# The first x tile's second slab by a DMA transpose, and W1's second block in another queue

## The chip, the cores and the metric

The kernel runs on one core of one Trainium2 chip. The core has five engines that run side by side and wait for one another through semaphores: TensorE (PE, with PEld for its weight loads), VectorE (DVE), ScalarE (ACT), GpSimd (POOL) and SyncE (SP). SP, ScalarE and POOL can issue DMAs; all DMAs of the core run on its 16 DMA engines. The metric is the time of one execution in device microseconds, lower is better. Times in this document are in microseconds unless something else is said.

## The reference

The input x has 2048 rows (tokens) of 640 features. Two branches are computed from it and mixed by a gate for each token:

```python
g = _sigmoid((x * gate_w).sum(-1, keepdims=True))
# branch A: a diagonal state-space layer with complex states
Bu = jnp.einsum("bld,pd->blp", x + 0j, B_bar)
for t in range(L):
    h = Lam_bar[None, :] * h + Bu[:, t, :]
y = 2.0 * jnp.einsum("blp,dp->bld", hseq, Cmat).real + x * Dskip[None, None, :]
# branch B: a dense layer with gelu, 640 -> 1728 -> 640
h = _gelu(jnp.einsum("bsd,df->bsf", x, w1) + b1)
b = jnp.einsum("bsf,fd->bsd", h, w2) + b2
out = g * a + (1 - g) * b
```

All inputs and the output are bfloat16.

## The kernel before, in words

The tokens are cut into four tiles of 512. For each tile TensorE computes the first dense layer (`m1`, L670: 13 column blocks of 128 of W1's 1728, five k steps each), the input projection of the states (`bproj`, L713), the second dense layer (L937, and L800 for the last tile) and the output projection of the states (L986, and L849 for the last tile). ScalarE evacuates the accumulators, with gelu for the dense layer. VectorE rotates and scans the states (`ssm`) and combines the branches.

TensorE contracts over partitions, so it needs x transposed, with the features on the partitions: `xT[q]` holds tile q as five slabs of 128 features by 512 tokens. Most slabs come from DRAM by a DMA transpose (`xtrans`, L340). For the first tile the slabs k < KN, here KN = 2, come in another way: the two plain loads `xna0` and `xna1` bring 256 tokens each of the first KN*128 features (L370), TensorE transposes them in blocks of 128 x 128 against an identity matrix (L426, `xt0` to `xt3`), and VectorE copies them from the accumulator bank into `xT[0]` (L432, `xc0` to `xc3`).

W1 comes in pieces. `w1load(k, queue, priority)` loads 128 rows (one k step) of the first 1024 columns, 256 KB: block 0 from ScalarE's queue (L387), blocks 1 to 4 from SP's. The remaining 704 columns follow in two loads of all rows (L378, 480 and 400 KB). After these, SP issues the transposed loads of the B weights, the next x tiles, W2 and the C weights. Each DMA has its own semaphore.

ScalarE's queue begins with W1's block 0, the single-row load `b1b` (the tail of b1, L391), and the loads of four sets of rows (Lambda's real and imaginary parts, log_dt, b1). They land in the tile `rows`, which TensorE transposes in one go (`cols`, L453). From these columns a serial chain on VectorE and ScalarE (L458, L463, L476, L483 to L497) makes the tables of the state rotation. The same columns hold b1, the bias of the gelu, so that the first gelu (L657) comes behind this chain in ScalarE's queue.

The first dense layer of the first tile has an order of its own, `m1_first` (L638 to L652). TensorE starts with six matmuls on constants (`warm`, L414), which need no data, then the transposes `xt0` and `xt1`, one more matmul on a constant (`fill`, L439), and then the first eight column blocks of W1, bank by bank, k step by k step. The k = 0 step of the first six blocks is done on token halves, first on tokens 0 to 255 and then on 256 to 511, since the halves of x arrive apart. Block 7 waits until bank 7, which the transposes use, is free.

```python
steps = [(0, jf, h) for h in range(2) for jf in range(6)] + [(k, jf, None) for k, jf in seq if k or jf > 5]
```

The order on each engine is not written out by hand. Each operation is recorded with `op(name, engine, duration, reads, writes, fn, prio)`, and a list scheduler (`Sched.order`) takes, on each engine, among the operations that are ready by its own estimated durations, the one with the lowest priority number. TensorE's main operations have running numbers from `pe_prio()`; others have fixed ones (20.5 for `cols`).

Of the kernel before, what the change touches and what calls it, by code (L numbers as in the profile page):

```python
# [184 lines left out]
def bass_gated_mix__ssm_conv_s5__dense_activation_gelu__prompt_kernel(  # L185
# [18 lines left out]
    _, S, D = A_x.shape  # L204
# [3 lines left out]
    KD = D // 128  # L208
# [17 lines left out]
    with ExitStack() as es:  # L226
# [4 lines left out]
        xT = [SB(f"xT_{i}", [128, KD, 512], BF16) for i in range(NQ)]  # L231
# [11 lines left out]
        cols = SB("cols", [128, 3 * KP + NF], FP32)  # L243
# [10 lines left out]
        ident = SB("ident", [128, 128], BF16)  # L254
# [53 lines left out]
        op = pr.op  # L308
# [17 lines left out]
        def d_mm(n):  # L326
            return n / 2400.0 + 0.004
# [31 lines left out]
        def w1load(k, eng, prio, reads=()):  # L359
            edges = [0] + ([WSPLIT[k] * 128] if k in WSPLIT else []) + [FW]  # L360
            for i, (f0, f1) in enumerate(zip(edges, edges[1:])):
                load(f"w1_{k}{i}", eng, f"l_w1{k}{i}", W1sb[:, k, f0:f1], B_w1[k * 128:(k + 1) * 128, f0:f1], [("w1", k, i)], prio=prio + 0.1 * i, lat=2.6, reads=reads)
# [1 line left out]
        def w1tok(k, jf):  # L364
            return ("w1", k, int(jf >= WSPLIT.get(k, NW)))

        KN = 2

        for h in range(2):
            load(f"xna{h}", "sp", f"l_xna{h}", xn[0][:, 2 * h:2 * h + 2, 0:KN * 128],  # L370
                 x2[h * 256:(h + 1) * 256, 0:KN * 128].rearrange("(c p) d -> p c d", p=128), [("xna", h)], 0.2 * h, dur=0.45, lat=2.0 + 0.4 * h)
        w1load(1, "sp", 1)
        for k in range(KN, KD):
            xtrans(0, range(k, k + 1), 2 * k, 1.15)
            w1load(k, "sp", 2 * k + 1)
        FM = FW + 3 * 128
        for i, (f0, f1) in enumerate(((FW, FM), (FM, F))):
            load(f"w1_r{i}", "sp", f"l_w1r{i}", W1sb[:, :, f0:f1], B_w1[:, f0:f1].rearrange("(k p) f -> p k f", p=128), [("w1", "r", i)], prio=20 + i, lat=5.0)  # L378
# [5 lines left out]
            return inc("pool", nc.gpsimd.memset(rows[:, :], 0.0))  # L384

        op("rz", "pool", 0.2, (), list(ROWS) + ["b1b", "rz"], f_rz, prio=-90)
        w1load(0, "act", -110, reads=["rz"])  # L387
        for i, (nm, (r0, src)) in enumerate(ROWS.items()):
            src = src.rearrange("(k p) -> k p", p=128)
            load(nm, "act", "l_" + nm, rows[r0:r0 + src.shape[0], :], src, [nm], prio=-100 + i, dur=0.4)  # L390
# [25 lines left out]

        op("warm", "pe", 2.7, (), [("bank", 4)], f_warm, prio=-1000)

        for i, (k, c0, c1) in enumerate(((0, 0, 2), (1, 0, 2), (0, 2, 4), (1, 2, 4))):
            bank = (7, 6, 7, 6)[i]  # L420
            pt = PS[bank][:, :].bitcast(BF16)[:, 0:(c1 - c0) * 128]

            def f_xt(k=k, pt=pt, c0=c0, c1=c1):
                t = None
                for c in range(c0, c1):
                    t = nc.tensor.transpose(pt[:, (c - c0) * 128:(c - c0 + 1) * 128], xn[0][:, c, k * 128:(k + 1) * 128], ident[:, :])  # L426
                return inc("pe", t)

            op(f"xt{i}", "pe", 0.11 * (c1 - c0), [("xna", c0 // 2), "ident"], [("bank", bank)], f_xt, prio=-990 + i if i < 2 else 3.1 + 0.1 * i)

            def f_xc(k=k, pt=pt, c0=c0, c1=c1):
                return inc("dve", nc.vector.tensor_copy(out=xT[0][:, k, c0 * 128:c1 * 128], in_=pt))  # L432

            op(f"xc{i}", "dve", 0.42, [("bank", bank)], [("xT", 0, k, c0)], f_xc, prio=-2000 + i)

        def f_fill():
            t = None
            for _ in range(1):
                t = nc.tensor.matmul(PS[3][:, 0:256], one.broadcast_to([128, 128]), one.broadcast_to([128, 256]), start=True, stop=True)  # L439
            return inc("pe", t)  # L440

        op("fill", "pe", 0.11, [("xna", 0), "ident"], [("bank", 3)], f_fill, prio=-900)

        XK0 = [[("xT", 0, k)] for k in range(KD)]
        XK0[0] = [("xT", 0, 0, 0), ("xT", 0, 0, 2)]
        XK0[1] = [("xT", 0, 1, 0), ("xT", 0, 1, 2)]
        XT = {q: [("xT", q, k) for k in range(KD)] for q in range(1, NQ)}
        XT[0] = [t for x in XK0 for t in x]

# [2 lines left out]
        def f_cols():  # L452
            return inc("pe", nc.tensor.transpose(psC, rows[:, :], ident[:, :]))  # L453

        op("cols", "pe", 0.3, list(ROWS) + ["b1b", "ident"], [("bank", 7)], f_cols, prio=20.5)

        def f_cols1():
            return inc("dve", nc.vector.tensor_copy(out=cols[:, :], in_=psC[:, 0:RT + 1]))  # L458
# [179 lines left out]
        def m1_first():  # L638
            late = [(0, NW - 1), (1, NW - 1)]
            seq = [(k, jf) for k in range(KD) for jf in range(NW) if (k, jf) not in late]  # L640
            i = seq.index((2, NW - 1))
            seq[i:i] = late
            steps = [(0, jf, h) for h in range(2) for jf in range(6)] + [(k, jf, None) for k, jf in seq if k or jf > 5]
            for k, jf, h in steps:
                t0, t1 = (0, 512) if h is None else (256 * h, 256 * h + 256)

                def f_mm(jf=jf, k=k, t0=t0, t1=t1):
                    return inc("pe", nc.tensor.matmul(PS[jf][:, t0:t1], W1sb[:, k, jf * 128:(jf + 1) * 128], xT[0][:, k, t0:t1],  # L648
                                                      start=(k == 0 and t0 == 0), stop=(k == KD - 1), skip_group_check=jf < 6))

                op(f"m1_0_{jf}_{k}_{t0}", "pe", d_mm(t1 - t0), (XK0[k] if h is None else XK0[k][h:h + 1]) + [w1tok(k, jf)], [("bank", jf)],
                   f_mm, prio=pe_prio())  # L652
            for jf in range(NW):
                ctr["bank"] += 1

                def f_ge(jf=jf):
                    return inc("act", nc.scalar.activation(Gl[0][:, jf, :], PS[jf][:, :], ACT.Gelu_apprx_tanh, bias=b1col[:, jf:jf + 1]))  # L657

                op(f"ge_0_{jf}", "act", d_act(512), [("bank", jf), "b1col"], [("gl", 0, jf)], f_ge, prio=10)
# [442 lines left out]
```

## Time and profile before

| | us |
|---|---|
| median of 3 runs | 212.86 (212.53 to 212.92) |
| the profiled execution | 212.88 |
| its span, first to last instruction | 211.6 |
| TensorE busy | 208.8 |
| VectorE busy | 190.1 |
| ScalarE busy | 103.1 |

The span is what the trace covers; the profiled execution's own time is 1.3 longer. Matmuls are pipelined, and the ends of their records are modelled, so consecutive matmuls overlap in the trace: the distance between two starts is what one costs. Operations of TensorE that the text names are found in the trace by their line: L414 the matmuls on constants, L426 the transposes of x, L439 the filler, L453 the transpose of the rows, L648 the first dense layer of the first tile for its first eight column blocks, L670 the rest of it. A DMA has two times: that of its issue on a queue, and that at which its data has landed.

### The profile page before, as it was taken

What the parts mean: (1) busy time and instruction counts of PE and PEld (TensorE: products, weight loads), DVE (VectorE), ACT (ScalarE), POOL (GpSimd) and SP (SyncE); (2) the same over time, 40 slices, a digit from 0 to 9 for tenths busy, and PEclk for the clock granted to TensorE, in tenths of its full rate; (3) what the DMA queues carried; (4) which work ended last, traced back from release to release, by engine and by line L of the source; (5) the groups of instructions that cost most, each with busy time, mean ns of one, the idle gap of its engine ahead of it and who ended that gap; (6) DMA issues with size and microseconds to landing.
All of it is one profiled execution on the core that took longest, in us unless ns stands there. A gap on an engine that the chain in (4) does not pass through costs nothing.

```text
span 211.6 us, 2759 instructions
## 1 busy us (share of the span) xinstructions
PE 208.8 (99%) x1106; PEld 105.2 (50%) x1106; DVE 190.1 (90%) x240; ACT 103.1 (49%) x177; POOL 4.2 (2%) x12
## 2 busy tenths in 40 slices
PE   8999999999999999999999999999999999999996
PEld 4544444444564444444464444444446444567775
DVE  2399999999999999999999999899999999499744
ACT  1399556678850353556680063456660027623330
POOL 1000000030000000000100000000010000000000
DMA  6999999999700020066174000007553000005251
GB/s 162 240 270 125 205 207 201 382 168 181 178 0 3 0 50 0 0 71 152 28 62 112 3 0 0 0 2 77 125 107 115 0 3 0 0 0 105 67 142 62
DMA packets 48536, 19.08 MB, mean 90 GB/s; under 512 B 41484, under 2 KB 47244, under 8 KB 48524
## 3 DMA queue, kind: packets, MB, share of 16 engines
q1 hardware_dynamic: 46720, 17.33, 39.8%
q0 software_dynamic: 1600, 1.32, 4.7%
q10 hardware_dynamic: 204, 0.27, 0.4%
q8 instruction: 8, 0.13, 0.3%
q14 instruction: 4, 0.03, 0.1%
HBM read 8.41 MB, written 2.63 MB: 52 GB/s over the span
## 4 chain that ended last, share of the span: by engine, by line
PE 99%; DVE 0%; issue 0%
PE ps L670 22%; PE ps L713 20%; PE ps L937 20%; PE ps L986 15%; PE ps L800 7%; PE ps L849 5%; PE ps L648 4%; PE ps L414 1%; PE ps L691 1%; PE ps L948 1%; PE ps L426 0%; PE ps L814 0%; DVE W1sb L883 0%; PE ps L439 0%; PE ps L453 0%
## 5 line engine op out<-in xcount | busy, mean ns | idle before, releaser
L670 PE MATMUL ps<-xT,W1sb 128*128 128x512 bf16 x220 | 48.1, 379 | 0.0
L753 DVE TENSOR_TENSOR_SCAN W<-atab,V 128x1280 bf16<-128x1280 f32 x16 | 44.3, 2811 | 0.3
L713 PE MATMUL ps<-xT,BT 128*128 128x512 bf16 x200 | 43.8, 379 | 0.0
L937 PE MATMUL ps<-Gl,W2sb 128*128 128x512 bf16 (+1 forms) x234 | 42.7, 344 | 0.0
L677 ACT ACTIVATE Gl<-ps,cols 128x512 bf16<-128x512 f32 x44 | 29.8, 695 | 15.5 <-PE ps L670 15.5
L670 PEld LDWEIGHTS ps<-xT,W1sb 128*128 128x128 bf16 x220 | 21.5, 98 | 26.0
L986 PE MATMUL ps<-Hb,CT 128*128 128x512 bf16 x150 | 32.9, 379 | 0.0
L937 PEld LDWEIGHTS ps<-Gl,W2sb 128*128 128x128 bf16 x234 | 22.9, 98 | 19.3
L713 PEld LDWEIGHTS ps<-xT,BT 128*128 128x128 bf16 x200 | 19.5, 98 | 23.7 <-ACT Gt L699 0.4
L722 ACT ACTIVATE U<-ps 128x512 bf16<-128x512 f32 x40 | 23.6, 596 | 14.8 <-PE ps L713 14.7
L955 ACT ACTIVATE E1T<-ps,cols 128x512 bf16<-128x512 f32 (+1 forms) x18 | 9.4, 624 | 36.0 <-PE ps L948 36.0
L986 PEld LDWEIGHTS ps<-Hb,CT 128*128 128x128 bf16 x150 | 14.5, 98 | 17.9 <-issue 0.6
L994 ACT ACTIVATE E2T<-ps 128x512 bf16<-128x512 f32 x15 | 9.1, 604 | 13.6 <-PE ps L986 13.6
L800 PE MATMUL ps<-W2sb,Gl 128*128 128x320 bf16 x104 | 14.8, 299 | 0.0
L622 DVE SCALAR_TENSOR_TENSOR trf<-xn,gwb 128x640 bf16<-128x640 bf16 x16 | 13.2, 823 | 0.4
L503 DVE TENSOR_TENSOR V<-V,W 128x1280 bf16<-128x1280 bf16 x16 | 12.5, 821 | 0.3
L503 DVE TENSOR_TENSOR Hb<-Hb,V 128x1280 bf16<-128x1280 bf16 x16 | 12.5, 821 | 0.3
L503 DVE TENSOR_TENSOR V<-mr,U 128x2560 bf16<-128x2560 bf16 x8 | 11.9, 1492 | 0.3
L800 PEld LDWEIGHTS ps<-W2sb,Gl 128*128 128x128 bf16 x104 | 10.1, 98 | 4.3 <-issue 0.3
L503 DVE TENSOR_TENSOR Hb<-c,W 128x2560 bf16<-128x2560 bf16 x8 | 11.9, 1490 | 0.2
L503 DVE TENSOR_TENSOR V<-s,W 128x2560 bf16<-128x2560 bf16 x8 | 11.9, 1484 | 0.0
L503 DVE TENSOR_TENSOR W<-mi,U 128x2560 bf16<-128x2560 bf16 x8 | 11.9, 1484 | 0.0
(93 smaller groups left out, 152.0 us busy)
## 6 DMA issues: line engine op xcount, KB each, us to landing
W2sb<-in_B_w_dram SPq DMA_DIRECT2D x1, 2080.0 KB, 8.9
out_dram<-xn SPq DMA_DIRECT2D x3, 640.0 KB, 4.8
xn<-in_A_x_dram POOLq DMA_DIRECT2D x2, 640.0 KB, 7.8
W1sb<-in_B_w_dram SPq DMA_DIRECT2D x4, 256.0 KB, 3.9
trf<-grow SPq DMA_DIRECT2D x3, 256.0 KB, 5.8
xn<-in_A_x_dram SPq DMA_DIRECT2D x1, 640.0 KB, 7.1
W1sb<-in_B_w_dram SPq DMA_DIRECT2D x1, 480.0 KB, 4.9
out_dram<-W1sb SPq DMA_DIRECT2D x3, 160.0 KB, 1.8
```

The lines of the kernel that those rows point to most:

```text
L503: return inc("dve", nc.vector.tensor_tensor(out=o, in0=a, in1=b, op=o_))
L622: t = inc("dve", nc.vector.scalar_tensor_tensor(out=scr[:, :], in0=xn[q % 2][:, c, :], scalar=1.0, in1=gwb[:, :], op0=ALU.mult, op1=ALU.mu ...
L670: t = nc.tensor.matmul(PS[bank][:, :], W1sb[:, k, jf * 128:(jf + 1) * 128], xT[q][:, k, :], start=(k == 0), stop=(k == KD - 1))
L677: return inc("act", nc.scalar.activation(Gl[q % 2][:, jf, :], PS[bank][:, :], ACT.Gelu_apprx_tanh, bias=b1col[:, jf:jf + 1]))
L713: t = nc.tensor.matmul(PS[bank][:, :], BT[:, ci, kd, k * 128:(k + 1) * 128], xT[q][:, kd, :], start=(kd == 0), stop=(kd == KD - 1))
L722: return inc("act", nc.scalar.activation(dst, src, ACT.Copy, scale=1.0 if ci == 0 else -1.0))
L753: t = inc("dve", nc.vector.tensor_tensor_scan(out=g[:, ci, :], data0=a, data1=v[:, ci, :], initial=0.0, op0=ALU.mult, op1=ALU.add))
L800: t = nc.tensor.matmul(PS[bank][:, 0:HALF], Gl[q % 2][:, jf, t4 * 128:(t4 + 1) * 128], W2sb[:, jf, cols], start=False, stop=False, skip_gr ...
L849: t = nc.tensor.matmul(PS[bank][:, 0:n], H[b % NHB][:, ci, k, s * 128:(s + 1) * 128], CT[:, ci, k, cols], start=(i == 0), stop=(i == 2 * K ...
L937: t = nc.tensor.matmul(PS[bank][:, 0:t1 - t0], W2sb[:, jf, d * 128:(d + 1) * 128], Gl[q % 2][:, jf, t0:t1], start=(jf == 0), stop=False)
L955: return inc("act", nc.scalar.activation(E1T[:, d, t0:t1], PS[bank][:, 0:t1 - t0], ACT.Identity, bias=cols2[:, 0, d:d + 1]))
L986: t = nc.tensor.matmul(PS[bank][:, :].rearrange("p (s t) -> p s t", s=2), CT[:, ci, k, d * 128:(d + 1) * 128], Hb[:, 2 * (q % 2):2 * (q % ...
```

## The change

KN goes from 2 to 1. The plain loads of the first tile bring only its first 128 features (64 KB each, in rows of 256 bytes, instead of 128 KB in rows of 512). The second slab, k = 1, comes by a DMA transpose in SP's queue, ahead of the transposes for k = 2 to 4. The remaining plain load of the first x tile (`xnb`) brings 512 features instead of 384.

W1's block 1 leaves SP's queue. It is issued by ScalarE, behind the single-row load `b1b` and ahead of the four loads of rows.

On TensorE two of four transposes go before the filler and two of four behind the third half column; both pairs that stay use bank 7. The filler is two matmuls instead of one. Seven column blocks instead of six are done on token halves at k = 0. `cols` gets priority 23.5 instead of 20.5; in the order that the scheduler makes, it stands behind the second matmul of k = 2 where it stood before the first. On VectorE two copies go. Near the end of the program VectorE's order also changes: the sum of token chunk 12 (two operations, L503) and the product of chunk 14 with the skip weights (L870) stand ahead of the last state block's four operations instead of behind them.

```diff
-        KN = 2
+        KN = 1
...
-        w1load(1, "sp", 1)
         for k in range(KN, KD):
             xtrans(0, range(k, k + 1), 2 * k, 1.15)
-            w1load(k, "sp", 2 * k + 1)
+            if k > 1:
+                w1load(k, "sp", 2 * k + 1)
...
-        w1load(0, "act", -110, reads=["rz"])
+        for k in range(2):
+            w1load(k, "act", -110 + 9.5 * k, reads=["rz"])
...
-        for i, (k, c0, c1) in enumerate(((0, 0, 2), (1, 0, 2), (0, 2, 4), (1, 2, 4))):
-            bank = (7, 6, 7, 6)[i]
+        for i, (k, c0, c1) in enumerate(((0, 0, 2), (0, 2, 4))):
+            bank = 7
...
-            op(f"xt{i}", "pe", 0.11 * (c1 - c0), [("xna", c0 // 2), "ident"], [("bank", bank)], f_xt, prio=-990 + i if i < 2 else 3.1 + 0.1 * i)
+            op(f"xt{i}", "pe", 0.11 * (c1 - c0), [("xna", c0 // 2), "ident"], [("bank", bank)], f_xt, prio=-990 + i if i < 1 else 3.1 + 0.1 * i)
...
-            for _ in range(1):
+            for _ in range(2):
                 t = nc.tensor.matmul(PS[3][:, 0:256], one.broadcast_to([128, 128]), one.broadcast_to([128, 256]), start=True, stop=True)
...
-        op("fill", "pe", 0.11, [("xna", 0), "ident"], [("bank", 3)], f_fill, prio=-900)
+        op("fill", "pe", 0.22, [("xna", 0), "ident"], [("bank", 3)], f_fill, prio=-900)
...
-        XK0[1] = [("xT", 0, 1, 0), ("xT", 0, 1, 2)]
...
-        op("cols", "pe", 0.3, list(ROWS) + ["b1b", "ident"], [("bank", 7)], f_cols, prio=20.5)
+        op("cols", "pe", 0.3, list(ROWS) + ["b1b", "ident"], [("bank", 7)], f_cols, prio=23.5)
...
-            steps = [(0, jf, h) for h in range(2) for jf in range(6)] + [(k, jf, None) for k, jf in seq if k or jf > 5]
+            steps = [(0, jf, h) for h in range(2) for jf in range(7)] + [(k, jf, None) for k, jf in seq if k or jf > 6]
```

More of the change, by code (lines that the diff above doesn't have):

```diff
@@ L648, in f_mm @@
                     return inc("pe", nc.tensor.matmul(PS[jf][:, t0:t1], W1sb[:, k, jf * 128:(jf + 1) * 128], xT[0][:, k, t0:t1],
-                                                      start=(k == 0 and t0 == 0), stop=(k == KD - 1), skip_group_check=jf < 6))
+                                                      start=(k == 0 and t0 == 0), stop=(k == KD - 1), skip_group_check=jf < 7))
                 op(f"m1_0_{jf}_{k}_{t0}", "pe", d_mm(t1 - t0), (XK0[k] if h is None else XK0[k][h:h + 1]) + [w1tok(k, jf)], [("bank", jf)],
```

## The prediction

> **What bounds the kernel now.** I read the page first, then the chain that ended last in order of time, then the timelines of SP's and ScalarE's queues with the DMA issues narrowed to one issue at a time, and last the stretches with the DMA share.
>
> ```profile
> span 211.6 us, 2759 instructions
> PE 208.8 (99%) x1106; PEld 105.2 (50%) x1106; DVE 190.1 (90%) x240; ACT 103.1 (49%) x177; POOL 4.2 (2%) x12
> ```
>
> TensorE is busy for the whole span. The chain, in order of time, begins so (start, length, what):
>
> ```profile
> 0.78 2.61 PE ps L414 x6
> 3.39 0.51 PE ps L426 x4
> 3.90 0.21 PE ps L439
> 4.11 0.78 PE ps L648 x3
> 4.89 0.43 PE ps L426 x4
> 5.32 2.98 PE ps L648 x17
> 8.29 0.06 PE ps L453
> 8.35 5.62 PE ps L648 x26
> 13.96 5.40 PE ps L670 x25
> ```
>
> The reader is to see that the chain never leaves TensorE: no load stands on it, so a load counts only when it becomes later than TensorE's need of it. The pieces also give prices. Four transposes (L426) take 0.43, so 0.107 each; the filler (L439) 0.21; 26 full matmuls 5.62, so 0.216 each. By the timeline, half-width matmuls start 0.213 apart until 5.75 and 0.109 apart afterwards: TensorE runs at half speed until 5.75. A saving before 5.75 therefore lets work move across that point at half its price.
>
> The two queues that the change reorders (SP, then ScalarE):
>
> ```profile
> 0.74 0.98 SPq L333 DMA_DIRECT2D xn<-in_A_x_dram  x2
> 1.76 0.47 SPq L333 DMA_DIRECT2D W1sb<-in_B_w_dram  x1
> 2.27 1.22 SPq L340 DMA_TRANSPOSE xT<-in_A_x_dram  x1
> 3.55 0.63 SPq L333 DMA_DIRECT2D W1sb<-in_B_w_dram  x1
> 4.23 1.13 SPq L340 DMA_TRANSPOSE xT<-in_A_x_dram  x1
> ```
> ```profile
> 1.40 1.18 ACTq L333 DMA_DIRECT2D rows<-in_B_b_dram  x1
> ```
>
> Issuing a transpose costs SP 1.1 to 1.2, a plain load about 0.5. The DMA issues, asked one at a time, tell how long after its issue a W1 block lands: block 0 (ScalarE, 0.97), block 2 (SP, 3.55), block 3 (SP, 5.40).
>
> ```profile
> W1sb<-in_B_w_dram ACTq DMA_DIRECT2D x1, 256.0 KB, 2.9
> W1sb<-in_B_w_dram SPq DMA_DIRECT2D x1, 256.0 KB, 4.2
> W1sb<-in_B_w_dram SPq DMA_DIRECT2D x1, 256.0 KB, 3.5
> ```
>
> Block 1 (1.76) takes 4.1 and block 4 (7.19) 3.7; the x transposes issued at 2.27, 4.23 and 6.03 take 4.3, 4.0 and 3.4. They are so long because the 16 DMA engines are full:
>
> ```profile
> 4.00:5.00 1.00, 1.00 (x7) 0.75 (x7) 0.22 (x2) 0.76 (x1) 0.00 (x0) 1.00 0.97 187
> 6.00:7.00 1.00, 1.00 (x9) 0.65 (x7) 0.00 (x0) 0.00 (x0) 0.00 (x0) 1.00 1.21 293
> ```
>
> The last two columns are DMA share and GB/s. So before, block 2 lands at 7.80 and its first matmul starts at 8.19: a cushion of 0.4, the thinnest on the path. A landing is usable about 0.15 later (block 0: landed 3.92, first matmul 4.07).
>
> **The change, part by part.** The sum is made against the profiled execution: 212.88, its span 211.6 and 1.3 around it that nothing here touches. It lies 0.02 over the median 212.86.
>
> 1. TensorE's own work. Before the switch to full speed, two of four transposes at 3.29 go and a second filler of equal length (0.213) takes their place: zero. Two of four transposes at 4.68 go (0.213 at half speed), and one more half column fits in before 5.75. After 5.75 the list is one half column longer (0.109) and one full matmul of block k=0 shorter (0.216). Net -0.11: the first matmul on block 1 moves from 6.62 to 6.51. At full speed throughout it would be -0.11 too, at half speed throughout -0.21.
>
> 2. Smaller first loads (64 KB instead of 128 each, in 256 B runs). The first transposes start at 3.29 just after their load (issued 0.74, 2.5 to landing, 3.24); the six warm-up matmuls hold TensorE until 3.19, so at most 0.10 at half speed, worth 0.05; and W1's block 0 at 3.92 holds the next step anyway. Range 0 to -0.05; I take -0.02. The Trainium skill speaks against even that: "DMA: Bandwidth & Descriptors", Specifications, wants runs of at least 512 B for line rate, by which halved runs gain nothing and this term is 0; no row here shows a 256 B run of a plain load.
>
> 3. First use of k=1 at 6.51. Its x slab, now a transpose issued at 1.76, lands after 3.4 to 4.3, at 5.2 to 6.1: in time. W1's block 1 goes to ScalarE behind the single-row load (1.40 to 2.58), so it is issued at 2.61 and lands after 2.9 (block 0, same queue) to 4.2 (SP), at 5.5 to 6.8; wanted at 6.36. Wait 0 to 0.45. I take none, going by the row of its own queue.
>
> 4. First use of k=2 at 8.02, two matmuls earlier in the list than the rows' transpose, which moves behind them. SP's order is now x, x, transpose, transpose, block 2: the second transpose is issued at 3.03, block 2 at 4.21 instead of 3.55. With 3.5 to 4.2 to landing it arrives at 7.71 to 8.46 and is wanted at 7.88: wait 0 to 0.58. The DMA work ahead of it grows by a transpose (128 KB) and shrinks by as much of x, but it no longer stands behind block 1 in SP's own queue. I take 3.8, between its own row and that of block 3: 8.01, a wait of 0.14. Behind a wait here stand the rows' transpose, two matmuls later, and the chain of step 6; both move with it.
>
> 5. Everything behind on SP is issued 0.63 later, a transpose (1.22) for a load (0.47) and its small gaps: W1's block 3 lands at about 9.5 for a use at 10.24, block 4 at 11.5 for 11.97, the first wide rest (issued 7.81, 4.9 to landing) at 13.3 for 13.69, the transposed B weights at 17.2 for 19.2, the second x tile about 26.3 for 30.15. The cushions after taking off 0.15 are 0.6, 0.3 and 0.2: cost 0. The other end is the row behind it, 5.6 to landing: 14.0, a wait of 0.5. The rest of x (512 KB instead of 384) and gate weights are wanted by VectorE at 49.6 and land near 31. POOL issues what it did.
>
> 6. The rows' transpose (L453) and what hangs on it. The four row loads leave ScalarE about 0.4 later, behind block 1's issue. The last was in by 8.13 at the latest; with 0.4 more it is in by 8.53 where the transpose is due at 8.46: wait 0 to 0.1, taken 0. Behind it runs a serial chain on VectorE and ScalarE with two activation-table loads, to the first gelu: 12.59 - 8.13 = 4.46 after it, and 0.69 for that gelu. TensorE needs its bank at L670, 5.67 after the transpose before, 5.24 now (two 0.216 less); the chain gives 4.46 + 0.69 + about 0.13 = 5.28. Cost 0.04; the cover that hid it is gone, so any later delay of the rows falls on TensorE at full price. If hand-over is quicker it is 0, at most 0.2.
>
> 7. VectorE loses two copies (0.29 each) in idle time: 0. Its tables start 0.33 later. TensorE wants the first states at 72.0, VectorE has them at 68.5: 3.5 of cover, cost 0. Near the end VectorE now does chunk 12's sum (two of 0.49, after an evacuation that ends at 194.9) and a product of 0.88 ahead of the last states. Those end about 201.3 instead of 197.9, wanted by TensorE at 203.97: cost 0, 2.6 of cover.
>
> Sum: -0.11 - 0.02 + 0.14 + 0.04 = +0.05, so 212.93; forecast 212.9, no change. I call no change what lies within 0.2% (0.43).
>
> **The rivals.**
>
> Slower, by block 2 of W1. Place: the first k=2 matmul. If the load keeps the 4.2 of its own row it lands at 8.46 and TensorE waits 0.58: -0.11 - 0.02 + 0.58 + 0.04 = +0.49, 213.4. It decides once the landing passes about 8.4. For it: full DMA engines, two transposes ahead. Against it: a shorter SP backlog, no block 1 in it. Block 1 late on ScalarE does not add to this, since a wait at k=1 moves the need at k=2 as well.
>
> Slower, by the wide rest of W1 at L670. With 5.6 to landing the wait is 0.5, in all 213.3 with the sum's other terms less the 0.14. For it: the full engines carry one transpose more, and the cushion is 0.2. Against: its own row, 4.9, is in time.
>
> Faster, by the clock. TensorE reached full speed at 5.75, 4.97 after its first matmul, with pauses near 3.2 and 4.0. If the new filler made that come at 4.7, half of 1.05 would be saved: 212.4. For it: steadier matmuls. Against: the filler only replaces transposes, so TensorE is as busy as before. The Trainium skill, "TensorE: Matmul & The Clock Gate", Part 1, has a free-running window of 3.4 us and a switch that varies by 0.5 either way from run to run; by it either kernel shifts by up to 0.25 and the change by nothing on average. The single profiled run cannot show that.
>
> The change does nothing but trade: if every load is in time, -0.09 or 212.8, still no change.
>
> **How the numbers follow.** No change 0.50 (waits adding to less than about 0.5), slower by block 2 or block 1 0.25, slower by the wide rest or by late rows 0.12, faster by the clock or an earlier start 0.13. Hence faster 0.13, same 0.50, slower 0.37. The range leaves out half of the faster cases and the worst of the slower, where a wait at k=2 meets one at L670: 212.5 to 213.5. The likeliest case alone spans 212.7 to 213.2.
>
> **What would show it.** The first k=1 matmul at 6.5 without idle before it (step 1, 3). The first k=2 matmul at 8.0 to 8.2; at 8.4 or more the first rival holds. The rows' transpose 0.3 to 0.5 later than 8.13, and the first L670 matmul within 0.1 of the end of the first gelu (step 6): if the gelu ends well earlier, step 6 is wrong. The switch of spacing from 0.213 to 0.109 at another time than 5.75 speaks for the clock. From L713 on, the pieces of the chain should have the same lengths as now; a longer piece there would make all of this wrong.

## The result and the profile after

The changed kernel takes 214.30 us (median of 22 runs, 213.83 to 215.41), the kernel before 212.89 in the same session (22 runs): the ratio is 1.0063, 95% interval 1.0049 to 1.0077. That is 1.4 us slower and outside the forecast range of 212.5 to 213.5.

The page's first lines, then the chain that ended last in order of time (start, length, what):

```profile
span 213.1 us, 2742 instructions
...
PE 207.7 (97%) x1090; PEld 104.4 (49%) x1104; DVE 189.7 (89%) x238; ACT 103.0 (48%) x177; POOL 4.2 (2%) x12
```
```profile
1.27 0.45 SPq L333
1.77 6.20 DMA xT<-in_A_x_dram
8.01 2.12 PE ps L648 x9
10.13 0.06 PE ps L453
...
13.04 2.32 PE ps L648 x10
15.36 5.45 PE ps L670 x25
20.82 3.02 PE ps L713 x14
```

Before, the chain never left TensorE. Now its first eight microseconds are two issues of SP's and one DMA: the transpose of slab 1, issued at 1.77, lands 6.20 later, and the first k=1 matmul starts at 8.01. From L670 to the end of the span nothing has changed: 211.6 - 13.80 = 197.8 before, 213.1 - 15.26 = 197.8 now (13.80 and 15.26 are the first L670 matmuls). The whole loss lies ahead of L670.

TensorE's timeline (start, length, line, operation; in brackets the idle time before it and what ended that):

```profile
3.46 0.63 PE L440 MATMUL ps<-const-bfloat16-1.0 128*128 128x256 bf16 x2
4.05 0.61 PE L648 MATMUL ps<-xT,W1sb 128*128 128x256 bf16 x3
5.45 0.28 PE L427 MATMUL ps<-ident,xn 128*128 128x128 bf16 x2 [0.78 <-DMA xn<-in_A_x_dram]
5.57 1.49 PE L648 MATMUL ps<-xT,W1sb 128*128 128x256 bf16 x11
8.01 2.12 PE L648 MATMUL ps<-xT,W1sb 128*128 128x512 bf16 x9 [0.96 <-DMA xT<-in_A_x_dram]
9.96 0.22 PE L453 MATMUL ps<-ident,rows 128*128 128x128 bf16 x1
10.02 5.34 PE L648 MATMUL ps<-xT,W1sb 128*128 128x512 bf16 x23
15.26 1.02 PE L670 MATMUL ps<-xT,W1sb 128*128 128x512 bf16 x4
```

The same stretch in the kernel before:

```profile
5.11 3.19 PE L648 MATMUL ps<-xT,W1sb 128*128 128x256 bf16 x17
8.13 0.22 PE L453 MATMUL ps<-ident,rows 128*128 128x128 bf16 x1
8.19 5.77 PE L648 MATMUL ps<-xT,W1sb 128*128 128x512 bf16 x26
13.80 5.56 PE L670 MATMUL ps<-xT,W1sb 128*128 128x512 bf16 x25
```

Two waits are new. The second half of x is late (its transposes start at 5.45), and slab 1 is late (8.01). Only the second counts, since the first lies ahead of it and the half columns were done by 6.9. Behind it, everything keeps its old distance: the first k=1 matmul is 1.39 later than before (8.01 against 6.62), the first k=2 matmul 1.34 (9.53 against 8.19), L670 1.46.

The DMA issues of the changed kernel, asked one at a time (x's second half at 1.27, slab 1 at 1.77, block 1 at 2.61, block 2 at 4.37; the last number is the time from issue to landing, called the lag below):

```profile
xn<-in_A_x_dram SPq DMA_DIRECT2D x1, 64.0 KB, 4.1
...
xT<-in_A_x_dram SPq DMA_TRANSPOSE x1, 6.2
...
W1sb<-in_B_w_dram ACTq DMA_DIRECT2D x1, 256.0 KB, 5.0
...
W1sb<-in_B_w_dram SPq DMA_DIRECT2D x1, 256.0 KB, 4.9
```

The forecast had 3.4 to 4.3 for slab 1 and 2.9 to 4.2 for block 1. Four loads that were issued in time are late together, so the question is what slowed them.

### The profile page after: what moved, and what is told of

Same layout as the page of the kernel before. It is cut to its first block, busy times and chain, and to the rows that moved or that the text cites. A ratio compares the mean times of both kernels' runs of the same rounds, so it can differ in the third digit from the quotient of the medians.

```text
span 213.1 us, 2742 instructions
## 1 busy us (share of the span) xinstructions
PE 207.7 (97%) x1090; PEld 104.4 (49%) x1104; DVE 189.7 (89%) x238; ACT 103.0 (48%) x177; POOL 4.2 (2%) x12
## 3 DMA queue, kind: packets, MB, share of 16 engines
HBM read 8.41 MB, written 2.63 MB: 52 GB/s over the span
## 4 chain that ended last, share of the span: by engine, by line
PE 95%; DMA 3%; issue 1%; SPq 0%; DVE 0%
PE ps L670 22%; PE ps L713 20%; PE ps L937 20%; PE ps L986 15%; PE ps L800 7%; PE ps L849 5%; PE ps L648 3%; DMA xT<-in_A_x_dram 3%; PE ps L691 1%; PE ps L948 1%; SPq L333 0%; PE ps L814 0%; DVE W1sb L883 0%; PE ps L453 0%
## 5 line engine op out<-in xcount | busy, mean ns | idle before, releaser
L670 PE MATMUL ps<-xT,W1sb 128*128 128x512 bf16 x214 | 47.3, 379 | 0.3
L713 PE MATMUL ps<-xT,BT 128*128 128x512 bf16 x196 | 43.3, 379 | 0.2
L670 PEld LDWEIGHTS ps<-xT,W1sb 128*128 128x128 bf16 x220 | 21.4, 98 | 26.1 <-issue 0.4
L503 DVE TENSOR_TENSOR Hb<-Hb,V 128x1280 bf16<-128x1280 bf16 x16 | 12.5, 822 | 0.3
L503 DVE TENSOR_TENSOR V<-V,W 128x1280 bf16<-128x1280 bf16 x16 | 12.5, 822 | 0.3
L503 DVE TENSOR_TENSOR V<-mr,U 128x2560 bf16<-128x2560 bf16 x8 | 11.9, 1492 | 0.4
L503 DVE TENSOR_TENSOR Hb<-c,W 128x2560 bf16<-128x2560 bf16 x8 | 11.9, 1490 | 0.2
L503 DVE TENSOR_TENSOR W<-mi,U 128x2560 bf16<-128x2560 bf16 x8 | 11.9, 1485 | 0.0
L503 DVE TENSOR_TENSOR V<-s,W 128x2560 bf16<-128x2560 bf16 x8 | 11.9, 1484 | 0.0
```

The costliest lines, as they stand in the source:

```text
L503: return inc("dve", nc.vector.tensor_tensor(out=o, in0=a, in1=b, op=o_))
L670: t = nc.tensor.matmul(PS[bank][:, :], W1sb[:, k, jf * 128:(jf + 1) * 128], xT[q][:, k, :], start=(k == 0), stop=(k == KD - 1))
L713: t = nc.tensor.matmul(PS[bank][:, :], BT[:, ci, kd, k * 128:(k + 1) * 128], xT[q][:, kd, :], start=(kd == 0), stop=(kd == KD - 1))
```

## The experiments

All ratios are to the kernel before, run on the same chip, with 95% intervals. "Slab 1" and "block 1" are the two loads for k=1. The figures of landings come from each run's profiled execution. TensorE's order is made anew by the scheduler for each kernel, and in some the rows' transpose stands earlier (ahead of the first k=1 matmul with block 1 last; ahead of the first k=2 matmul with slabs and blocks in turn and with block 1 behind slab 1 on SP). What the loads do is therefore read from their landings.

### First round: which of the two moves

Three theories: A, transposes that lead SP's queue hold up the rest; B, block 1 as a large load of a second queue does; C, the 256-byte runs of the first x loads do.

**Block 1 back to SP**, between the x loads and slab 1:

```diff
+        w1load(1, "sp", 1)
         for k in range(KN, KD):
...
-        for k in range(2):
-            w1load(k, "act", -110 + 9.5 * k, reads=["rz"])
+        w1load(0, "act", -110, reads=["rz"])
```

> The changed kernel with W1's block 1 back in SP's queue, between the plain loads of x and the transposes. Theory A (the slab transposes, first in SP's queue with nothing but the small x loads ahead, hold the DMA engines, so that the second half of x lands at 5.4 instead of 4.3 and the k=1 data at 7.6 to 8.0): x's second half lands by 4.4 again, the transposed slab k=1 at 6.5 to 7.2 (before, the first transpose in that place landed at 6.54), the first k=1 matmul at 6.7 to 7.3 instead of 8.01, time 212.9 to 213.6. Theory B (block 1 in ScalarE's queue shares the DMA engines with SP's transposes and both are drawn out): the same recovery, 212.7 to 213.3. Theory C (the 256-byte runs of the small x loads are slow): x's second half stays at 5.2 or later and the time at 214 or more.

Measured: 213.67, ratio 1.0033 (1.001 to 1.0055). x's second half landed at 3.94, block 1 at 5.83, slab 1 (issued 2.27) at 7.27, slab 2 at 7.98; first k=1 matmul 7.31. By the ratio, about half of the loss went.

**The kernel before with block 1 on ScalarE**, behind the single-row load:

```diff
-        w1load(1, "sp", 1)
...
-        w1load(0, "act", -110, reads=["rz"])
+        for k in range(2):
+            w1load(k, "act", -110 + 9.5 * k, reads=["rz"])
```

> The kernel before with only W1's block 1 moved to ScalarE's queue behind the single-row load; two slabs of x still by plain loads. Theory A: a transpose (k=2) now stands right behind the x loads, so the second half of x lands about 1 later than 4.26, block 1 at 7 or later, first k=1 matmul at 7.2 to 7.8 instead of 6.62, time 213.5 to 214.2. Theory B: the same or worse, since block 1 still shares the engines with a transpose. Theory C: no change, 212.7 to 213.1, as the x loads have 512-byte runs.

Measured: 215.04, ratio 1.0096 (1.0058 to 1.0134). Its TensorE timeline:

```profile
5.94 0.40 PE L426 MATMUL ps<-ident,xn 128*128 128x128 bf16 x4 [1.21 <-DMA xn<-in_A_x_dram]
6.18 1.48 PE L648 MATMUL ps<-xT,W1sb 128*128 128x256 bf16 x10
7.95 1.68 PE L648 MATMUL ps<-xT,W1sb 128*128 128x512 bf16 x7 [0.29 <-DMA W1sb<-in_B_w_dram]
```

This kernel has no transposed slab 1 at all, and it loses at least as much. Block 1 in ScalarE's queue is enough by itself; here it landed at 7.91, and slab 2 (issued 1.76) at 7.89.

**Slab 1 by a plain load.** The transposition of slab 1 is left out in this kernel (its content is then not x transposed), so that its time tells what the transpose costs:

```diff
-            xtrans(0, range(k, k + 1), 2 * k, 1.15)
+            (load("xT0_1", "sp", "l_xT0_1", xT[0][:, 1, :], x2[0:128, 0:512], [("xT", 0, 1)], 2 * k, dur=1.15, lat=3.0) if k == 1 else xtrans(0, range(k, k + 1), 2 * k, 1.15))
```

> The changed kernel with slab k=1 brought by a plain load of the same 128 KB into the same tile, in the same place of SP's queue; its transposition is left out, so that the slab's content is other data. Block 1 stays in ScalarE's queue. Theory A: x's second half lands by 4.5, block 1 and the slab by 6.3, the first k=1 matmul at 6.5 to 6.8, time 212.6 to 213.2. Theory B: block 1 still lands at 7 or later because the transpose for k=2 is in flight beside it, first k=1 matmul at 7.2 or later, 213.5 or more. Theory C: x's second half at 5.2 or later.

Measured: 214.64, ratio 1.0081 (1.0056 to 1.0106). The plain slab landed at 5.91, but block 1 at 7.69 and slab 2, the transpose now next in SP's queue, at 7.95. Taking one transpose away only let the next one into its place.

**First x loads in 512-byte runs:**

```diff
-            load(f"xna{h}", "sp", f"l_xna{h}", xn[0][:, 2 * h:2 * h + 2, 0:KN * 128],
-                 x2[h * 256:(h + 1) * 256, 0:KN * 128].rearrange(...
+            load(f"xna{h}", "sp", f"l_xna{h}", xn[0][:, 2 * h:2 * h + 2, 0:256],
+                 x2[h * 256:(h + 1) * 256, 0:256].rearrange(...
```

> The changed kernel with the two first x loads in 512-byte runs again (256 features each, 128 KB), of which only the first 128 features are used early; the rest load brings 384 features. Slab k=1 still by a transpose. Theories A and B: no recovery, x's second half at 5.2 or later, time 214.0 to 214.6. Theory C: x's second half at 4.3 to 4.6, time 213.3 or less.

Measured: 214.73, ratio 1.0089 (1.0056 to 1.0121); x's second half at 5.89, slab 1 at 7.60, block 1 at 7.44. Theory C falls. A and B each explain part of the round and neither all of it.

### Second round: the place of block 1

**The changed kernel with block 1 directly behind block 0**, ahead of the single-row load. One number changes; block 1 is issued at 1.40 instead of 2.61:

```diff
-            w1load(k, "act", -110 + 9.5 * k, reads=["rz"])
+            w1load(k, "act", -110 + k, reads=["rz"])
```

> The changed kernel with W1's block 1 in ScalarE's queue directly behind block 0, ahead of the single-row load, so issued at about 1.4 instead of 2.61. After the first four runs two theories are left. Theory A2 (while a slab transpose is in flight the DMA engines move little, whatever the queue; what is issued beside it or just ahead of it lands late): block 1 lands by 6.0 now, x's second half still at 4.8 or later and the slab k=1 at 6.8 to 7.8 because nothing large stands ahead of the transposes, first k=1 matmul at 7.0 to 7.9, 213.4 to 214.2. Theory B2 (large loads from two queues at once slow each other, transposes or not): block 1 at 7 or later, 214.2 or more.

Measured: 212.87, ratio 0.9998 (0.9978 to 1.0019). The whole loss is gone. TensorE's timeline marks no wait for a load; within the 20 matmuls, the first on k=2 stands 0.16 later than it could, behind block 2's landing at 7.43:

```profile
4.46 0.28 PE L427 MATMUL ps<-ident,xn 128*128 128x128 bf16 x2
4.57 3.59 PE L648 MATMUL ps<-xT,W1sb 128*128 128x256 bf16 x20
8.00 0.22 PE L453 MATMUL ps<-ident,rows 128*128 128x128 bf16 x1
8.05 5.34 PE L648 MATMUL ps<-xT,W1sb 128*128 128x512 bf16 x24
```

Block 1 landed at 4.88, slab 1 at 5.57 and slab 2 at 6.30, though both transposes stand where they stood. Theory A2, that leading transposes are late by themselves, missed; theory B2, that two queues' large loads slow each other, missed too, since block 1 is still in the second queue.

**The kernel before with block 1 directly behind block 0 on ScalarE:**

```diff
-        w1load(1, "sp", 1)
...
-        w1load(0, "act", -110, reads=["rz"])
+        for k in range(2):
+            w1load(k, "act", -110 + k, reads=["rz"])
```

> The kernel before with W1's block 1 in ScalarE's queue directly behind block 0 (about 1.4), both first slabs by plain loads. Theory A2: block 1 by 6.0, x's second half at 4.8 to 5.9 since the transpose for k=2 stands right behind it, first k=1 matmul at 6.8 to 7.8, 213.0 to 214.0: better than 215.04 with block 1 behind the single row. Theory B2: block 1 at 7 or later again, 214.5 or more.

Measured: 213.18, ratio 1.0008 (0.9982 to 1.0035), against 1.0096 with block 1 behind the single row. Here too both theories missed: x's second half came at 4.22, block 1 at 4.98, the slab (k = 2) at 5.60. The same place cures both kernels.

**All slabs by plain loads.** The transposition of slabs 1 to 4 is left out:

```diff
-            xtrans(0, range(k, k + 1), 2 * k, 1.15)
+            load(f"xT0_{k}", "sp", f"l_xT0_{k}", xT[0][:, k, :], x2[(k - 1) * 128:k * 128, 0:512], [("xT", 0, k)], 2 * k, dur=1.15, lat=3.0)
```

> The changed kernel with all four slabs k=1 to 4 of the first tile by plain loads of the same bytes into the same places, in the same order; their transposition is left out, so that these slabs hold other data. Block 1 stays in ScalarE's queue behind the single row. Theory A2: with no transpose in flight before the B weights, x's second half lands by 4.2, block 1 by 6.3, first k=1 matmul at 6.4 to 6.6 without a wait, 212.6 to 212.9. Theory B2: block 1 still at 7 or later, first k=1 matmul at 7.2 or later, 213.5 or more.

Measured: 213.69, ratio 1.0028 (1.0005 to 1.005). Slab 1 landed at 5.16 and block 1, issued at 2.62, at 6.55: a lag of 3.9, inside the forecast's 2.9 to 4.2, though later than the 6.3 that was expected here. The first k=1 matmul started at 6.93 without a wait. So block 1 behind the single-row load does little harm where no transpose is under way. (What makes up this kernel's loss is not settled; in this profile no load was waited for, and TensorE went to full speed late, at 6.7.)

**Block and slab in turn, all on SP** (block 1, slab 1, block 2, slab 2, ...):

```diff
+        w1load(1, "sp", 1)
...
-                w1load(k, "sp", 2 * k + 1)
+                w1load(k, "sp", 2 * k - 1)
...
-        for k in range(2):
-            w1load(k, "act", -110 + 9.5 * k, reads=["rz"])
+        w1load(0, "act", -110, reads=["rz"])
```

> The changed kernel with block 1 back in SP's queue and blocks and slab transposes taking turns there (block 1, slab 1, block 2, slab 2, and so on) instead of slab 1 and slab 2 back to back. If two transposes back to back are what drew slab 1 out to 7.27 in the run with block 1 back on SP: slab 1 at 6.5 to 6.9, first k=1 matmul at 6.7 to 7.0, then a wait for slab 2 until 8.2 to 8.4, 212.9 to 213.4. If each transpose alone takes that long: slab 1 at 7.2 or later and 213.6 or more.

Measured: 213.30, ratio 1.0015 (0.999 to 1.004). No wait at k=1; slab 1 (issued 2.27) landed at 6.46, and slab 2 at 8.06, in time. A wait of 0.65 came at L670 instead, where the wide rest of W1 landed at 14.57.

### Third round: time of issue, or the single-row load

**Three short loads ahead of block 1 instead of the single-row load**, so that it is issued at the same time (2.64):

```diff
-            w1load(k, "act", -110 + 9.5 * k, reads=["rz"])
+            w1load(k, "act", -110 + 12.5 * k, reads=["rz"])
...
-             B_b1[nmain:F]..., ["b1b"], prio=-101, dur=1.2)
+             B_b1[nmain:F]..., ["b1b"], prio=-96, dur=1.2)
```

> The changed kernel with other loads ahead of W1's block 1 in ScalarE's queue: three of the short loads of rows (0.36, 0.30 and 0.57 of issue) instead of the single-row load, which goes behind all of them. Block 1 is issued at about 2.65 as in the changed kernel. Theory 'time of issue': a 256 KB load that enters when two slab transposes are already under way, with no other large load ahead of it, comes late whatever stood ahead of it: it lands at 7 or later (a lag of 4.5 or more), x's second half after 5, the first k=1 matmul starts at 7.3 to 8.0, ratio to the kernel before 1.004 to 1.009. Theory 'single-row load': that load holds the queue or the engines: without it ahead block 1 lands at 5.5 to 6.3, the first k=1 matmul starts at 6.5 or before, ratio 0.998 to 1.001. Against the second: a delay of the row loads to about 6.5 is no wait in either theory, since the rows' transpose is due after 8.

Measured: 213.96, ratio 1.004 (1.0017 to 1.0063); slab 1 at 7.92, block 1 at 7.60, first k=1 matmul at 7.97. x's second half, at 4.81, was less late than the 5 that was expected. It is the time of issue; the single-row load costs only the 1.2 that ScalarE needs to issue it.

**Block 1 early on ScalarE, slab and block in turn on SP:**

```diff
-                w1load(k, "sp", 2 * k + 1)
+                w1load(k, "sp", 2 * k - 1)
...
-            w1load(k, "act", -110 + 9.5 * k, reads=["rz"])
+            w1load(k, "act", -110 + k, reads=["rz"])
```

> The changed kernel with block 1 directly behind block 0 on ScalarE (1.40) and, in SP's queue, slab and block in turn: slab 1, block 2, slab 2, block 3, slab 3, block 4, slab 4. Where transposes back to back draw each other out and late plain loads, block 2 (issued at about 3.05 instead of 4.25) lands at 6.5 to 7.0 instead of 7.43, slab 2 at 6.6 to 7.4 instead of 6.30, and the wait of 0.16 for block 2 at the first k=2 matmul goes: rows' transpose at 7.8 to 8.0, ratio to the kernel before 0.997 to 0.9995. Rival: two large plain loads ahead of slab 2 make it the last: it lands after 7.6, a wait of 0.2 to 0.6 at k=2, ratio 1.000 to 1.003.

Measured: 213.35, ratio 1.0005 (0.9985 to 1.0025). Block 2 came at 6.97 and the wait at k=2 went, as expected, but slab 2 landed at 7.69, past the expected 7.4, x's second half came at 5.19 in this profile, and the wide rest of W1 at 14.12, a wait of 0.30 at L670. No gain over the version with block 1 first alone.

**Block 2 in the early place on ScalarE, block 1 behind the single row** (issued 3.10):

```diff
-        for k in range(2):
-            w1load(k, "act", -110 + 9.5 * k, reads=["rz"])
+        for k, prio in ((0, -110), (2, -109), (1, -100.5)):
+            w1load(k, "act", prio, reads=["rz"])
...
-            if k > 1:
+            if k > 2:
                 w1load(k, "sp", 2 * k + 1)
```

> The changed kernel with block 2 (not block 1) directly behind block 0 on ScalarE at 1.40, and block 1 behind the single-row load, now at about 3.0; SP issues x, x, slab 1, slab 2, slab 3, block 3, slab 4, block 4. Theory 'early load' (what matters for x's second half and slab 1 is that some large plain load is under way before the transposes): x's second half lands by 4.4, slab 1 by 6.0, and only block 1 is late (6.5 to 7.7), which sets the first k=1 matmul; k=2 then waits for nothing; ratio 1.001 to 1.006. Theory 'late load' (block 1 entering behind the transposes takes the engines from what is already under way): x's second half lands after 5, slab 1 after 7.2, first k=1 matmul at 7.4 to 8.4, ratio 1.005 to 1.010.

Measured: 213.97, ratio 1.0062 (1.0037 to 1.0087). A split verdict: x's second half was in time (4.23), so an early large load protects it or leaves it alone; slab 1 was late all the same (7.55), with block 1 at 7.42. For slab 1 it is the late load that counts.

### Fourth round: mixture, and whose queue

**Block 1 last among ScalarE's loads** (issued 4.05):

```diff
-            w1load(k, "act", -110 + 9.5 * k, reads=["rz"])
+            w1load(k, "act", -110 + 15.5 * k, reads=["rz"])
```

> The changed kernel with W1's block 1 at the end of ScalarE's loads (behind the four loads of rows, issued at about 4.2 instead of 2.61), so that the slab transposes run without a large plain load beside them, and with none ahead of them but block 0. Theory 'mixture' (block 1 entering in the middle of the transposes draws both out): slab 1 lands by 5.7 (a lag of 3.9 or less, as with block 1 early), slab 2 by 6.7, x's second half by 4.4; block 1 alone is late, lands at 7.2 to 8.4 and sets the first k=1 matmul. Theory 'transposes alone' (they keep the engines slow whatever is beside them unless a large plain load is already under way): slab 1 lands at 7 or later though block 1 is not beside it, and x's second half after 5. The time is that of a first k=1 matmul at 7.4 to 8.6 in both: ratio to the kernel before 1.003 to 1.010.

Measured: 213.62, ratio 1.0047 (1.0031 to 1.0063). Slab 1 landed at 5.18, a lag of 3.4; slab 2 at 6.43; x's second half at 4.16; only block 1 came late (7.30), as it was issued late: its lag was 3.3. Two transposes back to back, with no large load ahead of them but block 0, are as quick as the forecast took them to be. Theory 'mixture' holds, 'transposes alone' falls.

What the engines did between 3.75 and 5.00 shows it. Packets by queue (q1 is SP's, q10 ScalarE's): count, MB, share of the 16 engines' time. The packets of 256 bytes are those of the slab transposes and of the first x loads; block 1 comes in packets of 2 KB. First the changed kernel, then block 1 last, then block 1 first:

```profile
q10 hardware_dynamic: 41, 0.08, 47.7%
q1 hardware_dynamic: 202, 0.05, 24.2%
```
```profile
q1 hardware_dynamic: 774, 0.19, 71.7%
q10 hardware_dynamic: 29, 0.00, 2.4%
```
```profile
q1 hardware_dynamic: 795, 0.19, 82.4%
q10 hardware_dynamic: 98, 0.13, 30.7%
```

In the same 1.25 us SP's queue (x's second half and the transposes) advances by 202 packets in the changed kernel and by 774 and 795 in the other two. Block 1's packets crawl as well: 0.477 x 16 x 1.25 / 41 = 0.23 us each. In the kernel with block 1 last they are slow at first too, until slab 2 is nearly in (6.43). The packets there between 5.25 and 6.00, then between 6.00 and 7.00:

```profile
q10 hardware_dynamic: 54, 0.10, 72.5%
q1 hardware_dynamic: 58, 0.01, 7.4%
```
```profile
q1 hardware_dynamic: 109, 0.20, 54.5%
q10 hardware_dynamic: 98, 0.17, 46.5%
```

The first 46 packets of 2 KB take 0.19 each, the 82 behind them 0.09 (0.465 x 16 / 82; the other 16 of the 98 are small ones). Over the whole load the trace gives 0.19 in the changed kernel, 0.12 with block 1 last and 0.09 with block 1 first. The stretch in which they ran tells the cases apart: 3.84 to 7.02 in the changed kernel, beside the transposes; 5.28 to 6.93 with block 1 last, when most of the transposes' packets had gone; 3.27 to 4.52 with block 1 first, ahead of most of them. So the engines do not share out a fixed rate: where the two lie side by side, both are slow. All of block 1 and slabs 1 and 2 had landed by 8.81 in the changed kernel, by 7.30 with block 1 last, by 6.30 with block 1 first.

**Slab and block in turn on SP, block 1 still at 2.62 on ScalarE:**

```diff
-                w1load(k, "sp", 2 * k + 1)
+                w1load(k, "sp", 2 * k - 1)
```

> The changed kernel with slab and block in turn on SP (slab 1, block 2, slab 2, block 3, slab 3, ...), block 1 still on ScalarE at 2.61: one transpose in flight when block 1 enters, and block 2 right behind it at 3.05. Theory 'back to back' (it takes two transposes in a row to draw a slab out): slab 1 lands by 6.2, block 1 by 6.5, first k=1 matmul by 6.7; ratio 0.999 to 1.003. Theory 'any transpose' (one in flight beside late plain loads is enough): slab 1 or block 1 lands at 7 or later, first k=1 matmul at 7.2 to 8.2; ratio 1.003 to 1.009.

Measured: 214.07, ratio 1.0067 (1.0042 to 1.0092); slab 1 at 7.69, block 1 at 7.50. One transpose under way is enough ('any transpose'):

```profile
7.74 1.69 PE L648 MATMUL ps<-xT,W1sb 128*128 128x512 bf16 x7 [0.69 <-DMA xT<-in_A_x_dram]
```

**The changed kernel again**, with no edit:

> The changed kernel itself, profiled a second time. If its first profile shows a property of the kernel: x's second half lands after 5 again, slab 1 and block 1 at 7.3 to 8.2, first k=1 matmul at 7.4 to 8.3. If the landings are chance of one execution: one of the three more than 0.8 earlier than before (5.40, 7.96, 7.64).

Measured: slab 1 at 7.90, block 1 at 7.59, first k=1 matmul at 7.94: the same within 0.07. x's second half came at 4.72 instead of 5.40. So the late slab and block are the kernel's; how late x's second half is differs from one execution to the next.

**Block 1 directly behind block 0, again**, with no edit:

> The kernel with block 1 directly behind block 0 on ScalarE, profiled a second time. If its first profile shows a property of the kernel: block 1 lands by 5.2, slab 1 by 6.0, no wait at k=1. If chance: slab 1 or block 1 at 6.5 or later.

Measured: block 1 at 5.04, slab 1 at 5.62, no wait at k=1; x's second half at 4.98 (4.31 the first time).

**Block 1 on SP directly behind slab 1** (issued 3.08), the last question, whether any plain load does it or one of the other queue:

```diff
-        for k in range(2):
-            w1load(k, "act", -110 + 9.5 * k, reads=["rz"])
+        w1load(0, "act", -110, reads=["rz"])
...
+            if k == 1:
+                w1load(k, "sp", 3)
             if k > 1:
                 w1load(k, "sp", 2 * k + 1)
```

> The changed kernel with W1's block 1 in SP's queue directly behind slab 1's transpose (issued at about 3.05), ahead of slab 2; the rest as in the changed kernel. Theory 'two queues' (the packets of two queues interleave on the engines, and a transpose is drawn out by a large plain load of the other queue): slab 1 lands by 5.8, block 1 behind it at 6.2 to 7.0, first k=1 matmul at 6.5 to 7.1; ratio to the kernel before 0.999 to 1.004. Theory 'any plain load' (a 256 KB load right behind a transpose draws it out whatever the queue): slab 1 lands at 7 or later, first k=1 matmul at 7.2 to 8.2; ratio 1.003 to 1.008.

Measured: 213.47, ratio 1.0027 (1.0006 to 1.0048). Slab 1 landed at 5.88 and block 1 at 6.55; the first k=1 matmul started at 6.69. Packets between 3.75 and 5.00:

```profile
q1 hardware_dynamic: 480, 0.14, 75.4%
q10 hardware_dynamic: 28, 0.00, 1.8%
```

'Two queues' holds for slab 1: the same load does no such harm from SP's own queue. It was issued 0.46 later than in the changed kernel, but that is not the reason: with block 2 in the early place, block 1 went out from ScalarE at 3.10, and slab 1 landed at 7.55. From SP's queue block 1's packets ran from 4.31 to 5.95, mostly behind the slab's. What the profile shows of the ratio that is left is a later wait: in this order block 2 landed at 8.41, the first matmul on it waited 0.30 behind the rows' transpose, and L670 began at 14.16 instead of 13.80.

### What they say together

Where block 1 was issued from ScalarE 0.3 to 1.3 after SP's first slab transpose, slab and block both landed between 7.4 and 8.0. That is so in eight profiles of seven kernels, whatever else they had: a plain slab 1, no separate slab 1, wide x loads, other loads ahead, other orders on SP. Issued 0.36 before the transpose (1.40 against 1.76), or 2.3 after it, or behind it in SP's own queue, the slab landed between 5.2 and 5.9. The distance between the issues is not the rule by itself: with block 1 last it was issued 0.98 behind slab 2's transpose, and neither was late (lags of 3.4 and 3.3); there its packets came when most of the transposes' had gone. The cause is thus the large plain load of the other queue entering while the transposes' packets are under way. What stays open: why this mixture is slow in the engines (the traces show packet times, not what a packet waits for), and why slab 1 took 5.0 in the first experiment, where block 1 preceded it in its own queue, against 4.2 with blocks and slabs in turn. No version beat the kernel before: the two best, with block 1 directly behind block 0, are equal to it within their intervals.

The Trainium skill, "DMA: Bandwidth & Descriptors", section "Issuing engines are not separate DMA queues", says that DMAs of all issuing engines run on the same 16 engines and interleave, and that issuing from several only saves the sequencer's time. The runs agree with the first half: packets of both queues lie side by side in the windows above. They do not bear out the second: the same load sent from ScalarE (2.61) or from SP behind the slab (3.08) had slab 1 landing at 7.96 or at 5.88, far more than the 0.58 that SP needs to issue it.

## Why the prediction was wrong

**Step 1, TensorE's own work (-0.11).** Too small to be seen alone. The version with block 1 first is the trade without the late loads: the sum's other terms would give a ratio of 1.0002, and 0.9998 (0.9978 to 1.0019) agrees with that but could not tell it from no gain at all.

**Step 2, smaller first loads (-0.02).** The first load landed at 3.22 in the first profile of the changed kernel and 2.82 in the second, and the first transposes started at 3.27 behind it and at 3.19 behind the warm-up matmuls, which hold them from there on as the step had it. Wider runs brought nothing.

**Step 3, first use of k=1. This is the step that failed.** It said that slab 1 lands after 3.4 to 4.3 and so "in time" and that block 1 goes "by the row of its own queue", wait 0 to 0.45, taken none. The wait came out at 8.01 - 6.51 = 1.50 against the step's own time. Both lags were outside their ranges: 6.2 for slab 1 (3.4 to 4.3) and 5.0 for block 1 (2.9 to 4.2). (A landing was usable 0.05 later, 7.96 against 8.01, not the 0.15 of the prediction; that is small beside it.) The rows were good measurements of other situations: block 0 enters when only the first x load is under way, and in the kernel before every large load behind the first transpose is in the transpose's own queue. The ranges were even right where the mixture is missing: 3.4 (block 1 last) and 3.8 (block 1 first) for slab 1, 3.5 (block 1 first) and 3.9 (no transposes) for block 1. No row showed a transpose with a large load of another queue entering beside it, and the step should have widened its range for that. Nor do full engines, which the prediction gave as the reason for long lags, tell the cases apart: between 4 and 5 and between 6 and 7 the share of the engines' time was 0.97 and 1.21 before and 0.80 and 1.69 in the changed kernel, while what they moved fell in both, from 187 and 293 GB/s to 118 and 127.

The late x half was not priced at all. It cost nothing in the changed kernel, since slab 1 came later still: in the second profile it was 0.68 earlier, the first k=1 matmul 0.07.

**Step 4, first use of k=2 (0.14).** Block 2 took 4.9 (3.5 to 4.2 was said) and landed at 9.28, and nobody waited, since the need had moved to 9.53. The sentence under the first rival, that a wait at k=1 moves the need at k=2 as well, was right. With block 1 first, where k=1 is in time, the wait for block 2 was 0.16 in one profile, near the 0.14 that was taken, but by luck: block 2's lag was 3.1, below the range, and TensorE came to it early, at 7.41. In the second profile of that kernel there was no wait.

**Step 5, everything behind on SP (0).** The cost held: blocks 3 and 4 at 10.00 and 11.17, the wide rest at 12.68, the B weights at 17.23, all ahead of needs that had moved by 1.4. The issues moved by 0.82, not 0.63 (the step's own 1.22 for 0.47 makes 0.75), as the two transposes in a row held SP's queue for 1.25 and 1.26. The cushion of the wide rest is thin, as the step said: the two orders that brought it later (14.57 and 14.12) waited for it.

**Step 6, rows' transpose and gelu (0.04).** Held to a hundredth or two. The first gelu started 4.46 after the rows' transpose, as before (9.97 and 14.43), and the first L670 matmul stood 0.06 behind its cover, a gap found at 0.05 to 0.06 in seven other kernels with this order of TensorE. It is the part of the 1.46 at L670 that the 1.39 at k=1 leaves, nearly.

**Step 7, VectorE (0).** Held: from L670 on the span is equal.

**The rivals.** "Slower, by block 2" had the right sign and the wrong load: the late loads were slab 1 and block 1, at k=1, and the price 1.4 instead of 0.49. The chance of 0.25 named block 1 as well, but no term and no rival had slab 1 late. The wide rest decided nothing here. "Faster, by the clock" cannot be told from one profile: TensorE's spacing fell at 4.3 in the first profile of the changed kernel and at 5.9 in the second, and k=1 began at 8.01 and 7.94. Where a load decides, an early clock gains nothing.

## What to carry to other kernels

Price a load that moves to another queue by what will be under way on the engines when it enters, not by an earlier row of that queue. Here a 256 KB load that entered from the other queue 0.3 to 1.3 us behind the first of several DMA transposes cost both of them; it did no such harm ahead of the transpose, or behind it in the same queue. A scarce early slot in a queue is best not spent behind a small load that takes 1.2 us to issue: here the order of two loads on ScalarE was worth the whole 1.4 us.

## What the runs showed of the hardware

- Mixture: a 128x512 slab transpose landed 3.4 after its issue with no large load entering for 2.3 behind it, 3.8 behind a large load that entered earlier, and 5.8 to 6.2 with a 256 KB load of the other queue entering 0.85 later. The engines moved 155, 263 and 108 GB/s between 3.75 and 5.00 in block 1 last, block 1 first and the changed kernel.
- TensorE's switch to full speed fell between 3.5 and 6.7 over the profiles of the study, and 1.6 apart in two executions of the same kernel. The Trainium skill, "TensorE: Matmul & The Clock Gate", Part 1, has it vary from run to run; the spread here is wider than the 0.5 either way that the prediction took from it. Single profiles differ by it. The medians were needed for another reason too: the kernel before with block 1 first had the shortest span, 210.8, yet that execution took 213.11, 2.3 more than its span.
- Outside the span the profiled execution of the kernel before spent 1.3, but 24 of the 96 executions that ran beside the experiments spent 1.9 to 2.5. So did 6 of 14 of its two versions; of the 126 of the changed kernel and its versions none spent more than 1.6. What fills that time was not found. It makes the changed kernel's versions look better by the ratio than by the span, most of all in the third round: block 1 early with slab and block in turn has a ratio of 1.0005, but a median span of 212.05 against 211.40. With block 1 directly behind block 0 the spans agree as the ratio does, 211.50 against 211.40.
